# Loading one value weight in a thin and a wide column piece, and the first value projections by row blocks

## The chip, the cores and the metric

The kernel runs on one core of a Trainium2 chip. The core has five instruction streams that run side by side: TensorE (PE in the profile; its weight loads are listed as PEld), VectorE (DVE), ScalarE (ACT), GpSimd (POOL) and SyncE (SP). They meet through semaphores. Loads from memory are issued as DMAs from SyncE's or ScalarE's instruction stream and moved by 16 DMA engines that all streams share. The metric is the device time of one execution in microseconds (us); less is better.

## What is computed

The input `x` has 2048 rows of 512 columns, in bf16. Each row is normalized, and the result goes into two branches that are added to `x`.

```python
xn = layernorm(x)                                  # 2048 x 512
q, k, v = split(xn @ wqkv)                         # 32 heads of 16 columns each
phi(t) = [softmax(t @ w_phi), softmax(-t @ w_phi)] # per head, 32 features
kv = phi(k)^T v ;  z = sum over rows of phi(k)
o  = (phi(q) kv) / (phi(q) z + 1e-6)
A  = o @ wo                                        # linear attention
B  = ((xn @ w_gate) * (xn @ w_up)) @ w_down        # 1792 hidden columns
out = x + A + B
```

## The kernel before

The 2048 rows are 16 row tiles of 128 rows, numbered 0 to 15, and four groups of four. In the code `n` is a row tile, and `c` or `j` is one of the four blocks of 128 input columns (DC is 4). The weight for v is the last third of `wqkv`. It lies on chip as `wv[128, 4, 512]`: `wv[:, j, :]` holds its rows 128 j to 128 j + 127, which is what the j-th matmul of a row tile reads. P is 128, D is 512, DH is 16.

All matrix products of a row tile need the tile transposed: `xnT` holds, for each column block, 128 columns of the input down the partitions and the rows along. The first four tiles are transposed on TensorE (`lt`, line 202: four 128x128 transposes into one PSUM bank, then one copy by ScalarE into `xnT`), the other twelve by DMA later on.

**The order of the work** is written out by hand: the engines' streams hold the instructions in the order in which the code issues them, and an instruction that waits holds up all behind it on its engine. The stretch around the change is the start of the kernel, in this order on each engine:

- SyncE issues the loads, lines 82 to 95: x tile 0, x tile 2, wv's column blocks j = 0, 1 (`dma_wv(0, 2)`), wv's j = 2, 3 (`dma_wv(2, DC)`), then pieces of the gate and up weights, `w_phi`, a transposing load of the k weights, and so on.
- ScalarE issues x tile 1 and x tile 3 (lines 102 and 103). Its first computation that waits for data is line 376, which sums each row of x tile 1 into `tots[1]`. Behind it in its stream stand the copies of the transposed tiles (line 206), two for tile 0 (each of two column blocks) and one for each of tiles 1 to 3.
- VectorE sums tile 0 (line 373) and writes `xns[0]` = 512 x minus its row sum in two halves (line 337); then `xns[1]`, which needs ScalarE's sum; then sum and difference of tile 2 and of tile 3; then the variances of the four tiles (line 340).
- TensorE starts with eight matmuls on constants (`warm_up`, line 311; the last one is a quarter as long), so that it is in use before data is there. Then come the transposes and the first value projections, `first_v(n, js)` (line 353): `first_v(n, js)` adds, for row tile n, the matmuls of the column blocks js into one PSUM bank. Tiles 0 and 1 use the two banks that later gather `kv`; tiles 2 and 3 take one of six rotating banks.

The order on TensorE is that of lines 380 to 397:

```python
lt(0, 0, 2); lt(0, 2, DC)
warm_up(2, 1)
first_v(0, (0,))
lt(1)
first_v(0, (1,))
lt(2)
first_v(0, (2, 3))
first_v(1, range(DC))
lt(3)
first_v(2, range(DC))
first_v(3, range(DC))
```

That is 16 matmuls of 512 columns and 16 transposes. Behind them follow `ffn(3)`, three units of eight matmuls each (lines 274 and 278), which read the gate and up weights and `xnT` of all four tiles, and then the rest of the kernel, some 206 us of mostly TensorE work.

Of the kernel before, what the change touches and what calls it, by code (L numbers as in the profile page):

```python
# [21 lines left out]
def kernel(  # L22
# [12 lines left out]
    nc = tc.nc  # L35
    P = 128
    S, D = A_x.shape[-2], A_x.shape[-1]
    F = B_w_gate.shape[-1]
    H = 32
    DH = D // H  # L40
    NT = S // P
    DC = D // P
# [15 lines left out]
    wv = wpool.tile([P, DC, D], BF16)  # L58
# [9 lines left out]
    def dma_x(lo, hi, eng=nc.sync):  # L68
        eng.dma_start(out=xall[:, lo:hi, :], in_=x_view[:, lo:hi, :])  # L69
# [1 line left out]
    def dma_cols(eng, w, src, lo, hi, at=0):  # L71
        eng.dma_start(out=w[:, :, lo - at:hi - at], in_=src[:, lo:hi].rearrange("(c p) f -> p c f", p=P))

    def dma_wv(lo, hi):
        nc.sync.dma_start(out=wv[:, lo:hi, :],
                          in_=A_wqkv[lo * P:hi * P, 2 * D:3 * D].rearrange("(c p) f -> p c f", p=P))

    def dma_gu(lo, hi):
        dma_cols(nc.sync, wg, B_w_gate, lo, hi)
        dma_cols(nc.sync, wu, B_w_up, lo, hi)  # L80

    dma_x(0, 1)
    dma_x(2, 3)
    dma_wv(0, 2)
    dma_wv(2, DC)
    dma_gu(0, 2 * P)
    nc.sync.dma_start(out=wphi[:], in_=A_w_phi.rearrange("(c h) d f -> (h d) c f", c=DC))
    dma_gu(2 * P, 5 * P)
# [10 lines left out]
    ones = nc.const_aps.tensor(1.0, [P, P], BF16)  # L99
    first = consts.tile([P, 1], BF16)  # L100
    nc.scalar.activation(out=first[:], in_=ones[:, 0:1], func=AF.Exp, scale=1.0)
    dma_x(1, 2, nc.scalar)
    dma_x(3, 4, nc.scalar)
    ident = consts.tile([P, P], BF16)
    make_identity(nc, ident[:])
    mhalf = consts.tile([P, GT], F32)
# [38 lines left out]
    def bank(name, dt=F32, n=TT):  # L145
        return ps_s.tile([P, n], dt, name=name, tag="s")
# [55 lines left out]
    def lt(n, lo=0, hi=DC):  # L202
        tp = bank("tp", BF16).rearrange("p (c t) -> p c t", c=DC)
        for c in range(lo, hi):
            nc.tensor.transpose(out=tp[:, c, :], in_=xns[n][:, c * P:(c + 1) * P], identity=ident[:])  # L205
        nc.scalar.copy(out=xnT[:, lo:hi, n * P:(n + 1) * P], in_=tp[:, lo:hi, :])  # L206
# [27 lines left out]
    def proj(ps, n, w, js=range(DC)):  # L234
        for j in js:
            nc.tensor.matmul(ps, lhsT=xnT[:, j, n * P:(n + 1) * P], rhs=w[:, j, :],  # L236
                             start=(j == 0), stop=(j == DC - 1))
# [68 lines left out]
    def warm_up(k, reps=DC):  # L306
        for _ in range(k):
            nc.tensor.matmul(warm[:, 0:reps * P], lhsT=ones,
                             rhs=nc.const_aps.tensor(1.0, [P, reps * P], BF16), start=True, stop=True)
# [4 lines left out]
    with tc.tile_pool(name="ps_k", bufs=1, space=PSUM) as ps_k:  # L314
# [21 lines left out]
        def sub_sum(n, tot, lo=0, hi=D):  # L336
            nc.vector.tensor_scalar(out=xns[n][:, lo:hi], in0=xall[:, n, lo:hi], scalar1=float(D), scalar2=tot[:],
                                    op0=ALU.mult, op1=ALU.subtract)
# [14 lines left out]
        def first_v(n, js):  # L353
            if n not in vps:
                vps[n] = kvbank[n][:] if n < 2 else bank("pv")
            proj(vps[n], n, wv, js)
# [15 lines left out]
        def sum_of(n):  # L372
            nc.vector.tensor_reduce(out=tots[n][:], in_=xall[:, n, :], axis=AX.X, op=ALU.add)
# [5 lines left out]
        sub_sum(1, tots[1])  # L379
        lt(0, 0, 2)  # L380
        lt(0, 2, DC)
        warm_up(2, 1)
        first_v(0, (0,))
        lt(1)
        first_v(0, (1,))
        for n in (2, 3):
            sum_of(n)
            sub_sum(n, tots[n])
        lt(2)
        first_v(0, (2, 3))  # L390
        first_v(1, range(DC))
        lt(3)
        first_v(2, range(DC))
        for n in (2, 3, 0, 1):
            stats_of(n)
            scales_of(n, float(D))
# [125 lines left out]
```

## Time and profile before

| what | value |
|---|---|
| time, median of 3 runs (lowest to highest) | 221.18 us (221.09 to 223.44) |
| time of the profiled execution | 221.23 us |
| its span, first to last instruction | 219.5 us |
| TensorE busy | 214.5 us, 98% of the span |
| VectorE, ScalarE, GpSimd busy | 141.0, 89.4, 74.1 us |
| granted TensorE clock | 0.999 |
| TensorE idle between 4.71 and 5.97 us | 1.26 us |

The profile shows one execution. Times within it count from its first instruction, and the measured time is 1.7 us longer than the span. A row of the timeline gives the start, the length of the stretch, the engine, the line of the kernel, the operation, what it writes and reads, the shapes, the count, and, in brackets, how long the engine had been idle before it and what ended that. A row with a count above 1 is a run of instructions that overlap or follow one another. A matmul of 512 columns has a latency of 379 ns in the profile, while the next one starts 216 ns later, so lengths overlap. DMA rows give the kilobytes and the time from issue to landing.

### The profile page before, as it was taken

The page shows a single profiled execution, that of the slowest core. Times are in us where ns is not written, and L with a number is a line of the kernel's source. Part 1 is how long each engine was busy: PE and PEld are TensorE (multiplying, and loading weights), DVE is VectorE, ACT ScalarE, POOL GpSimd, SP SyncE. Part 2 cuts the span into 40 slices and gives each one's busy share as a digit, 9 for nine tenths or more (in the row PEclk, how much of TensorE's full clock was granted, in tenths as well). Part 3 has the DMA queues.
Part 4 walks back from the last instruction along what each step waited for, and adds up shares of the span by engine and source line. Part 5 has one row for each costly group of instructions (what it writes and reads, how often), then busy time and mean ns, then how long its engine had stood idle before and what let it go on. Part 6 is the DMA issues. An engine that isn't in the chain of part 4 may idle for free.

```text
span 219.5 us, 3489 instructions
## 1 busy us (share of the span) xinstructions
PE 214.5 (98%) x1292; PEld 102.8 (47%) x1292; DVE 141.0 (64%) x239; ACT 89.4 (41%) x159; POOL 74.1 (34%) x71
## 2 busy tenths in 40 slices
PE   6999999999999999999999999999999999999994
PEld 2444445454444444444544444444444444444443
DVE  5858866886598757667499773196655645454321
ACT  5546586459665875465434222141231322100000
POOL 2540853363348463636045433033023033000000
PEclk9999999999999999999999999999999999999999
DMA  5999996102202431202018445114451431512301
GB/s 176 283 293 371 375 242 93 42 0 51 48 0 49 50 75 21 48 3 48 1 30 98 92 106 115 47 24 96 96 75 24 96 72 27 97 48 72 74 25 48
DMA packets 48529, 19.91 MB, mean 91 GB/s; under 512 B 37504, under 2 KB 48512, under 8 KB 48512
## 3 DMA queue, kind: packets, MB, share of 16 engines
q1 hardware_dynamic: 48224, 19.42, 39.8%
q10 hardware_dynamic: 288, 0.26, 0.4%
q8 instruction: 10, 0.16, 0.3%
q14 instruction: 7, 0.06, 0.1%
HBM read 8.67 MB, written 2.10 MB: 49 GB/s over the span
## 4 chain that ended last, share of the span: by engine, by line
PE 96%; DMA 2%; SPq 0%; DVE 0%; issue 0%
PE g L274 22%; PE fin L290 22%; PE u L278 22%; PE fin L293 6%; PE k L236 6%; PE q L236 6%; PE pv L236 6%; DMA wv<-in_A_wqkv_dram 2%; PE kv L330 2%; PE ab L461 2%; PE kv L236 1%; PE pq L225 1%; SPq L69 0%; PE tp L205 0%; DVE o_sb L300 0%
## 5 line engine op out<-in xcount | busy, mean ns | idle before, releaser
L274 PE MATMUL g<-xnT,wg 128*128 128x512 bf16 x224 | 57.5, 379 | 0.0
L278 PE MATMUL u<-xnT,wu 128*128 128x512 bf16 x224 | 57.5, 379 | 0.0
L282 DVE TENSOR_TENSOR hT<-u,g_sb 128x512 bf16<-128x512 f32 x56 | 37.0, 666 | 24.9 <-PE u L278 16.8
L253 POOL TENSOR_TENSOR phiq<-e,rsum 128x1024 bf16<-128x1024 f32 x16 | 30.9, 1933 | 63.5 <-DVE rsum L251 56.0
L281 ACT CAST g_sb<-g 128x512 bf16<-128x512 f32 x56 | 32.8, 587 | 47.1 <-PE g L274 46.9
L249 DVE TENSOR_REDUCE sums<-e 128x64 f32<-128x1024 f32 x32 | 38.9, 1216 | 20.1 <-ACT e L246 20.1
L290 PE MATMUL fin<-wd,hT 128*128 128x512 bf16 (+2 forms) x238 | 51.1, 366 | 0.0
L253 POOL TENSOR_TENSOR phik<-e,rsum 128x1024 bf16<-128x1024 f32 x16 | 30.9, 1932 | 40.6 <-DVE rsum L251 38.5
L278 PEld LDWEIGHTS <-wu 128*128 128x128 bf16 x224 | 21.9, 98 | 26.4
L290 PEld LDWEIGHTS <-hT 128*128 128x128 bf16 x238 | 22.4, 98 | 24.8
L274 PEld LDWEIGHTS <-wg 128*128 128x128 bf16 x224 | 21.1, 98 | 24.0
L236 PEld LDWEIGHTS <-xnT 128*128 128x128 bf16 x192 | 17.4, 97 | 18.4 <-ACT xnT L206 0.9
L300 DVE TENSOR_TENSOR o_sb<-fin,xall 128x512 bf16<-128x512 f32 (+2 forms) x13 | 8.5, 650 | 20.5 <-PE fin L293 20.5
L251 DVE RECIPROCAL rsum<-sums 128x64 f32<-128x64 f32 x32 | 17.7, 553 | 3.1
L293 PE MATMUL fin<-wo,oT 128*128 128x512 bf16 (+2 forms) x68 | 16.6, 366 | 0.0
L236 PE MATMUL k<-W1k,xnT 128*128 128x512 bf16 x64 | 16.4, 379 | 0.0
L236 PE MATMUL q<-W1q,xnT 128*128 128x512 bf16 x64 | 16.4, 378 | 0.0
L245 ACT ACTIVATE e<-q 128x512 f32<-128x512 f32 x12 | 7.2, 597 | 22.2 <-PE q L236 22.2
L236 PE MATMUL pv<-wv,xnT 128*128 128x512 bf16 x56 | 14.2, 379 | 0.0
L474 DVE TENSOR_TENSOR otok<-ab,rden 128x512 bf16<-128x512 f32 x16 | 11.1, 692 | 0.6
L322 ACT CAST vt<-pv 128x512 bf16<-128x512 f32 x12 | 7.0, 587 | 10.0 <-PE pv L236 10.0
L153 DVE BATCH_NORM_STATS2 stats<-xall 128x6 f32<-128x512 bf16 x16 | 10.6, 665 | 0.0
(61 smaller groups left out, 130.4 us busy)
## 6 DMA issues: line engine op xcount, KB each, us to landing
out_dram<-o_sb SPq DMA_DIRECT2D x15, 128.0 KB, 2.0
wd<-in_B_w_down_dram SPq DMA_DIRECT2D x1, 1792.0 KB, 15.6
xall<-in_A_x_dram SPq DMA_DIRECT2D x1, 1024.0 KB, 11.6
wg<-in_B_w_gate_dram SPq DMA_DIRECT2D x1, 640.0 KB, 8.6
wu<-in_B_w_up_dram SPq DMA_DIRECT2D x1, 640.0 KB, 9.8
wv<-in_A_wqkv_dram SPq DMA_DIRECT2D x2, 256.0 KB, 4.4
xall<-in_A_x_dram SPq DMA_DIRECT2D x1, 512.0 KB, 4.2
wg<-in_B_w_gate_dram SPq DMA_DIRECT2D x1, 512.0 KB, 5.4
```

The source lines that it names most:

```text
L153: nc.vector.bn_stats(out=stats[:], in_=xall[:, n, :])
L236: nc.tensor.matmul(ps, lhsT=xnT[:, j, n * P:(n + 1) * P], rhs=w[:, j, :], start=(j == 0), stop=(j == DC - 1))
L249: nc.vector.tensor_reduce(out=sums[:], in_=ev, axis=AX.X, op=ALU.add)
L251: nc.vector.reciprocal(out=rsum[:].rearrange("p a b -> p (a b)"), in_=sums[:])
L253: nc.gpsimd.tensor_tensor(out=phi[:].rearrange("p g (x f) -> p (g x) f", f=DH), in0=ev, in1=rsum[:].to_broadcast((P, 2 * H, DH)), op=ALU.mult)
L274: nc.tensor.matmul(gps, lhsT=wg[:, c, f * P:(f + 1) * P], rhs=xnT[:, c, T * TT:(T + 1) * TT], start=(c == 0), stop=(c == DC - 1))
L278: nc.tensor.matmul(ups, lhsT=wu[:, c, f * P:(f + 1) * P], rhs=xnT[:, c, T * TT:(T + 1) * TT], start=(c == 0), stop=(c == DC - 1))
L281: nc.scalar.copy(out=g_sb[:], in_=gps)
L282: nc.vector.tensor_tensor(out=hTs[T][:, f, :], in0=ups, in1=g_sb[:], op=ALU.mult)
L290: nc.tensor.matmul(ps, lhsT=hTs[T][:, f, t4 * P:(t4 + 1) * P], rhs=wd[:, f, lo:lo + w], start=(f == 0), stop=False)
L293: nc.tensor.matmul(ps, lhsT=oTs[n][:, c, :], rhs=wo[:, c, lo:lo + w], start=False, stop=(c == DC - 1))
L474: nc.vector.tensor_tensor(out=o_tok[:].rearrange("p (b h d) -> p b h d", b=2, d=DH), in0=abv[:, :, :, 0:DH], in1=rden[:].to_broadcast((P, ...
```

## The change

The load of `wv` is cut by columns as well. Columns 0 to 15 of all four column blocks (512 runs of 32 bytes) are one DMA, issued first in ScalarE's queue, ahead of x tile 1. The remaining 496 columns are loaded by SyncE in two halves as before. x tile 3 moves from ScalarE's queue to SyncE's. SyncE's order becomes x tile 0, wv's j = 0, 1 (columns 16 on), x tile 2, x tile 3, wv's j = 2, 3 (columns 16 on), and then the same loads as before. On TensorE the first projections are ordered by row blocks of `wv`: j = 0, 1 of tiles 0, 1 and 2, then j = 2, 3 of the same tiles. The two short warm-up matmuls of 128 columns behind tile 0's transposes become one of 512 columns.

```diff
-    def dma_wv(lo, hi):
-        nc.sync.dma_start(out=wv[:, lo:hi, :],
-                          in_=A_wqkv[lo * P:hi * P, 2 * D:3 * D].rearrange("(c p) f -> p c f", p=P))
+    def dma_wv(lo, hi, f0, f1, eng=nc.sync):
+        eng.dma_start(out=wv[:, lo:hi, f0:f1],
+                      in_=A_wqkv[lo * P:hi * P, 2 * D + f0:2 * D + f1].rearrange("(c p) f -> p c f", p=P))
...
     dma_x(0, 1)
+    dma_wv(0, 2, DH, D)
     dma_x(2, 3)
-    dma_wv(0, 2)
-    dma_wv(2, DC)
+    dma_x(3, 4)
+    dma_wv(2, DC, DH, D)
     dma_gu(0, 2 * P)
...
     nc.scalar.activation(out=first[:], in_=ones[:, 0:1], func=AF.Exp, scale=1.0)
+    dma_wv(0, DC, 0, DH, nc.scalar)
     dma_x(1, 2, nc.scalar)
-    dma_x(3, 4, nc.scalar)
...
         lt(0, 0, 2)
         lt(0, 2, DC)
-        warm_up(2, 1)
+        warm_up(1)
         first_v(0, (0,))
         lt(1)
         first_v(0, (1,))
+        first_v(1, (0, 1))
         for n in (2, 3):
             sum_of(n)
             sub_sum(n, tots[n])
         lt(2)
-        first_v(0, (2, 3))
-        first_v(1, range(DC))
+        first_v(2, (0, 1))
+        for n in range(2):
+            first_v(n, (2, 3))
         lt(3)
-        first_v(2, range(DC))
+        first_v(2, (2, 3))
         for n in (2, 3, 0, 1):
             stats_of(n)
             scales_of(n, float(D))
```

## The prediction

> **What bounds the kernel now.** I read the busy times of the whole span first, then busy times by stretch, then the waits of the first 11 us, then the timeline of the start engine by engine.
>
> ```profile
> span 219.5 us, 3489 instructions
> ...
> PE 214.5 (98%) x1292; PEld 102.8 (47%) x1292; DVE 141.0 (64%) x239; ACT 89.4 (41%) x159; POOL 74.1 (34%) x71
> ```
>
> ```profile
> 0.00:4.71 4.71, 3.81 (x14) 1.36 (x14) 2.11 (x11) 2.48 (x6) 1.59 (x9) 1.00 0.54 158
> 4.71:5.97 1.26, 0.00 (x0) 0.10 (x1) 1.22 (x3) 0.37 (x2) 0.00 (x0) 1.00 0.94 300
> 5.97:10.10 4.13, 4.12 (x29) 2.10 (x29) 3.54 (x10) 2.26 (x4) 2.27 (x6) 1.00 1.20 305
> 10.10:217.00 206.90, 206.55 (x1251) 99.27 (x1249) 134.13 (x217) 84.29 (x150) 70.25 (x56) 1.00 0.39 84
> ```
>
> Behind the bounds and the length of a stretch stands PE's busy time. PE is the bound: from 10.10 us, where the first `ffn` matmul starts, it is busy 206.55 of 206.90 us. Nothing behind that point can absorb a delay, and the change touches only what lies ahead. So the forecast is one number: when does that first `ffn` matmul start? Before, at 10.10. From 5.97 on, PE does not stop; its one real hole is 4.71 to 5.97, and it waits there for wv:
>
> ```profile
> PE kv L236 <- DMA wv<-in_A_wqkv_dram: 1.3, 1, 1.3
> ```
>
> PE's timeline:
>
> ```profile
> 5.97 0.38 PE L236 MATMUL kv<-wv,xnT 128*128 128x512 bf16 x1 [1.26 <-DMA wv<-in_A_wqkv_dram]
> 6.19 0.38 PE L205 MATMUL tp<-ident,xn 128*128 128x128 bf16 x4
> 6.41 0.38 PE L236 MATMUL kv<-wv,xnT 128*128 128x512 bf16 x1
> 6.63 0.39 PE L205 MATMUL tp<-ident,xn 128*128 128x128 bf16 x4
> 6.85 1.46 PE L236 MATMUL kv<-wv,xnT 128*128 128x512 bf16 x6
> 8.14 0.39 PE L205 MATMUL tp<-ident,xn 128*128 128x128 bf16 x4
> 8.37 1.89 PE L236 MATMUL pv<-wv,xnT 128*128 128x512 bf16 x8
> ```
>
> Paces: eight matmuls from 8.37 to 10.10 give 0.216 us each; four transposes from 8.14 to 8.37 give 0.22.
>
> The row that matters most is how soon a transposed tile can be used. PE's weight loads and ScalarE's timeline:
>
> ```profile
> 4.86 0.10 PEld L236 LDWEIGHTS <-xnT 128*128 128x128 bf16 x1 [0.33 <-ACT xnT L206]
> ...
> 7.25 0.56 PEld L236 LDWEIGHTS <-xnT 128*128 128x128 bf16 x4 [0.30 <-ACT xnT L206]
> ...
> 9.21 0.56 PEld L236 LDWEIGHTS <-xnT 128*128 128x128 bf16 x4 [0.30 <-ACT xnT L206]
> ```
>
> ```profile
> 3.31 0.63 ACT L376 ACTIVATE junk<-xall 128x512 bf16<-128x512 bf16 x1 [1.03 <-DMA xall<-in_A_x_dram]
> 3.85 0.19 ACT L376 ACTIVATION_READ_ACCUMULATOR junk<-xall 128x1 f32 x1
> 4.44 0.65 ACT L206 COPY xnT<-tp 128x256 bf16<-128x256 bf16 x2 [0.40 <-PE tp L205]
> ```
>
> Tile 1's transposes start at 6.19 and its first weight load, held by ScalarE's copy, is at 7.25; tile 3's are 8.14 and 9.21. So 1.07 us pass, 1.09 with 0.02 to the matmul. **Before, this lag is filled**: behind tile 1's transposes stand one matmul, tile 2's transposes and two matmuls (0.22 + 0.22 + 0.22 + 0.43 = 1.09); behind tile 3's stand their own 0.22 and four matmuls (1.08).
>
> **The change, part by part.**
>
> *The order on PE.* PE takes its stream in order. Call *a* the start of tile 1's transposes. Afterwards tile 1's transposes and tile 0's j = 1 fill 0.43 of the 1.09 up to tile 1's first matmul: a hole of 0.66. Two matmuls (0.43), then tile 2's transposes at a + 1.52. Directly behind stands tile 2's j = 0, which needs them: 1.09 again, 0.22 filled, a hole of 0.87; the ready matmuls of tiles 0 and 1 (j = 2, 3) are queued behind it. Then six matmuls (1.30) to tile 3's transposes at a + 3.91. Behind these only two matmuls remain before tile 3 itself: 1.09 with 0.22 + 0.43 filled, a hole of 0.44. Tile 3's four matmuls take 0.86. The first `ffn` matmul is thus at **a + 5.86**; the new holes sum to 1.97 us, against 1.26 that could be won. To break even, *a* would have to be 4.24.
>
> *When is a?* Ahead of it stands tile 0's j = 0 (0.22), which needs wv's j = 0 and tile 0's first copy. ScalarE issues that copy behind the row sum of x tile 1. With x1 landing at L: sum starts L + 0.02 (landed 0.84 + 2.4, started 3.31), ends 0.73 later (3.31 to 4.04), copy 0.03 on, weight load 0.42 after the copy's start (4.44 to 4.86), matmul 0.03 on: L + 1.23, and a = L + 1.45. Even with x1 as before, the copy starts at 4.44 after the transposes, so the matmul is at 4.89 and a = 5.11 at best: `ffn` at 10.97, 0.87 late. VectorE is not later than this: `xns[1]` is ready 0.5 us after the sum; tile 2's sum and difference take 1.1 us more and have 1.5.
>
> *x1's landing.* ScalarE's queue issues the 16 columns first:
>
> ```profile
> wphi<-in_A_w_phi_dram SPq DMA_DIRECT2D x1, 16.0 KB, 5.1
> ```
>
> This load of `w_phi` has the same form (512 runs of 32 bytes), and its issue takes 0.51 us on SP's timeline. x1 is then issued at about 1.38 instead of 0.84. Lower bound of L: 3.3, as before, if the DMA engines and not the issue set it. Nearest upper row: x tile 3, today second in this queue behind 128 KB, issued at 1.25, landed 2.9 later at 4.15; with 0.13 more, 4.3. What is ahead of x1 now is 16 KB, in 512 packets of 9 ns each in the packet records of `w_phi` over 16 engines, so 0.3 us per engine. I take 4.0 (3.8 from the issue alone, 4.3 from x3). Then a = 5.45, `ffn` at **11.31, 1.2 us late**.
>
> [...]
>
> *wv's landing.* Before it was issued at 1.71 and landed 4.2 later at 5.94. Now its first half is second in SP's queue, issued at 1.24 (0.47 sooner), with x2's and x3's 256 KB no longer ahead: some 0.8 us at the 305 GB/s of the stretches' rows. Between 4.7 and 5.5; tile 0's first matmul is not ready before 5.23, so I take it as hidden, and it costs up to 0.3 if not. PE's first projection now waits for two DMAs, with all of PE's stream behind it. The second half of wv is needed at a + 4.0, after 9; it landed at 6.7 before.
>
> *The rest.* SP issues one more load (x3, 0.45 us) ahead of all later ones. The first gate weights landed at 7.6 for a use at 10.1, the k weights at 12.8 for a use at 15.4; each has over 2 us of cover, and PE is later too. One warm-up matmul of 0.22 instead of 0.11 lies in PE's hole: nothing. Statistics and copies of the projections move with PE.
>
> **Sum.** 221.23 + 1.2 = 222.4 us; the profiled execution lies 0.05 above the median, which I leave out.
>
> **Rivals.**
>
> 1. *Forecast, the holes of the new order* (0.63): +0.9 to +1.6, 222.4.
> 2. *Data late as well* (0.20). PE would be held by wv or x1. If wv still landed at 5.94, a = 6.19 and `ffn` at 12.05, +1.95. If x1 slipped to 5.0, because the first touch of wv's rows now goes ahead of it in its queue, a = 6.45, +2.2. Around 223.3. For: wv took 4.2 us where x1 took 2.4. Against: it had more ahead of it.
> 3. *PE's clock falls* (0.05). At the start, seven warm-up matmuls step by 0.43 us (0.82 to 3.77), twice the 0.216 later, for some 3.3 us. Three holes in 6 us could bring that back for as long: +1.2 + 1.65, 224.1. Against: the hole of 1.26 before did not. [...]
> 4. *Faster* (0.06): the wait for wv goes and no hole replaces it, 221.23 − 1.26 = 220.0. It needs *a* under 4.24, or the lag of 1.09 well under 0.7; against it stand the weight loads at 7.25 and 9.21, both held by ScalarE's copy.
> 5. *Nothing* (0.06): holes and gain cancel, 221.2.
>
> **Range and chances.** 221.4 to 223.5 holds the forecast with both ends of L and nearly all of rival 2; rivals 3, 4 and 5 are left out. A difference of 1% (2.2 us) is about what a measurement of this kernel can tell from no change. Forecast, 4 and 5 are within it, 3 is over it, 2 about half: slower by over 1% 0.15, faster by over 1% 0.02, within 0.83.
>
> **What would show it.** Right: PE's first projection between 5.1 and 5.6, released by ScalarE's copy; then three holes of about 0.66, 0.87 and 0.44 ended by `xnT` copies; first `ffn` matmul near 11.3; behind it the same 206.9 us to the same point. Wrong: that matmul at or before 10.1, a first projection still held by wv, matmul steps of 0.43 behind 5 us, or a new wait of PE past `ffn`.

## The result, and the profile after

The changed kernel is slower: a median of 223.15 us over 22 runs (222.84 to 225.51) against 221.86 us for the kernel before over 22 runs beside it (220.91 to 223.44). The ratio is 1.0083, with a 95% interval of 1.0056 to 1.0110. The two medians differ by 1.29 us; the ratio, taken on the median shown before the prediction, 221.18, is about 1.8 us. The forecast was 1.2.

Both kernels' times fall into groups. The changed kernel has 12 runs from 222.8 to 223.2, 4 from 224.0 to 224.4 and 6 from 225.4 to 225.5. The kernel before has 11 from 220.9 to 221.6, one at 222.2 and 10 from 222.8 to 223.4. What the groups are was the second question of this study. Group against group the loss is larger than the medians say: the lowest group has a median of 222.93 after and 221.24 before, 1.69 us apart. The profiled execution of the changed kernel is one of its longest, 225.51 us. Its page, first lines:

```profile
span 223.8 us, 3465 instructions
...
PE 217.2 (97%) x1267; PEld 103.9 (46%) x1291; DVE 141.1 (63%) x239; ACT 89.4 (40%) x159; POOL 74.1 (33%) x71
```

The span is 4.3 us longer. The waits of its first 20 us have no entry for wv any more. In its place stand TensorE's waits for ScalarE's copies of the transposed tiles, and ScalarE's wait for x tile 1 has grown from 1.0 us to 2.4 (total, times, longest):

```profile
ACT junk L377 <- DMA xall<-in_A_x_dram: 2.4, 1, 2.4
...
PE kv L237 <- ACT xnT L207: 0.8, 2, 0.5
...
PE pv L237 <- ACT xnT L207: 0.7, 1, 0.7
```

TensorE's timeline of the same execution:

```profile
5.70 0.61 PE L237 MATMUL kv<-wv,xnT 128*128 128x512 bf16 x1 [0.54 <-ACT xnT L207]
6.10 0.63 PE L206 MATMUL tp<-ident,xn 128*128 128x128 bf16 x4
6.53 0.63 PE L237 MATMUL kv<-wv,xnT 128*128 128x512 bf16 x1
7.42 1.03 PE L237 MATMUL kv<-wv,xnT 128*128 128x512 bf16 x2 [0.25 <-ACT xnT L207]
8.24 0.63 PE L206 MATMUL tp<-ident,xn 128*128 128x128 bf16 x4
9.56 1.03 PE L237 MATMUL pv<-wv,xnT 128*128 128x512 bf16 x2 [0.68 <-ACT xnT L207]
10.38 1.91 PE L237 MATMUL kv<-wv,xnT 128*128 128x512 bf16 x4
12.09 0.63 PE L206 MATMUL tp<-ident,xn 128*128 128x128 bf16 x4
```

Two things show at once. Two of the three holes of the new order are there, ahead of the rows at 7.42 and 9.56, each ended by a copy (line 207 is the old 206). And four matmuls from 10.38 take 1.91 us to the end of the last one, 1.71 us to the next row: 0.43 us each instead of 0.22. TensorE is at half rate up to about 13 us. The first `ffn` matmul starts at 14.28 instead of 10.10, and from there to the last matmul of the kernel 206.34 us pass in both profiles (to 220.62 after, to 216.43 before). So nothing behind the start changed, and the start is 4.18 of the 4.28 us between these two executions.

Two more profiled executions of the changed kernel followed, without an edit.

> The changed kernel once more, for another profiled execution. Theory (holes and late x tile 1 at full clock, the clock on top in some executions): at 222.9 us matmul steps of 0.22 us from 6 us on and the first ffn matmul at 11.7 to 11.8; at 224.1 steps of 0.43 us for part of the stretch and that matmul near 13.0; behind it 206.3 us to the last matmul in each. Rival: another wait behind the first ffn matmul makes the difference between the times.

> The same again: the first ffn matmul at 11.7 to 11.8 in an execution at 222.9 us, near 13.0 at 224.1, near 14.3 at 225.4, and 206.3 us behind it; by the rival another wait behind that matmul.

One took 224.30 us, the other 223.01. The second is the changed kernel at full clock from its first projection on. Its TensorE timeline:

```profile
5.75 0.39 PE L237 MATMUL kv<-wv,xnT 128*128 128x512 bf16 x1 [0.65 <-ACT xnT L207]
5.98 0.39 PE L206 MATMUL tp<-ident,xn 128*128 128x128 bf16 x4
6.20 0.38 PE L237 MATMUL kv<-wv,xnT 128*128 128x512 bf16 x1
7.04 0.61 PE L237 MATMUL kv<-wv,xnT 128*128 128x512 bf16 x2 [0.46 <-ACT xnT L207]
7.49 0.39 PE L206 MATMUL tp<-ident,xn 128*128 128x128 bf16 x4
8.55 0.60 PE L237 MATMUL pv<-wv,xnT 128*128 128x512 bf16 x2 [0.68 <-ACT xnT L207]
8.99 1.03 PE L237 MATMUL kv<-wv,xnT 128*128 128x512 bf16 x4
9.86 0.39 PE L206 MATMUL tp<-ident,xn 128*128 128x128 bf16 x4
10.08 0.59 PE L237 MATMUL pv<-wv,xnT 128*128 128x512 bf16 x2
10.92 1.04 PE L237 MATMUL pv<-wv,xnT 128*128 128x512 bf16 x4 [0.25 <-ACT xnT L207]
11.79 1.03 PE L275 MATMUL g<-xnT,wg 128*128 128x512 bf16 x4
```

By the starts, with 0.22 us for a matmul or four transposes, the holes are 6.42 to 7.04, 7.71 to 8.55 and 10.51 to 10.92: 0.62, 0.84 and 0.41. The first `ffn` matmul is at 11.79. In the execution of 224.30 us it is at 13.06. There TensorE was at full rate, lost it, and got it back:

```profile
6.21 0.38 PE L237 MATMUL kv<-wv,xnT 128*128 128x512 bf16 x1
...
9.00 1.04 PE L237 MATMUL pv<-wv,xnT 128*128 128x512 bf16 x2 [0.68 <-ACT xnT L207]
9.83 1.46 PE L237 MATMUL kv<-wv,xnT 128*128 128x512 bf16 x4
11.13 0.39 PE L206 MATMUL tp<-ident,xn 128*128 128x128 bf16 x4
```

The last matmul comes 206.34 us behind the first `ffn` matmul in both. The three groups of the changed kernel are therefore 11.8, 13.1 and 14.3 us of start, and what separates the three profiled executions is how long TensorE runs at half rate. The clock records kept with the traces give the times: in the 225.51 us execution full rate came only at 13.32 us; in the 224.30 us execution it came at 3.87, was gone from 7.29 to 10.70, and came back; in the 223.01 us execution no step behind 5.75 is at half rate.

### The profile page after: what moved, and what is told of

The parts are those of the page before. It is cut to its first block, busy times and chain, and to the rows that moved or that the text cites. A ratio compares the mean times of both kernels' runs of the same rounds, so it can differ in the third digit from the quotient of the medians.

```text
span 223.8 us, 3465 instructions
## 1 busy us (share of the span) xinstructions
PE 217.2 (97%) x1267; PEld 103.9 (46%) x1291; DVE 141.1 (63%) x239; ACT 89.4 (40%) x159; POOL 74.1 (33%) x71
## 4 chain that ended last, share of the span: by engine, by line
PE 95%; DMA 1%; ACT 1%; issue 1%; DVE 0%
PE u L279 22%; PE fin L291 22%; PE g L275 21%; PE fin L294 6%; PE q L237 6%; PE k L237 6%; PE pv L237 6%; PE ab L464 2%; PE kv L331 2%; PE kv L237 1%; DMA xall<-in_A_x_dram 1%; ACT xnT L207 1%; PE tp L206 1%; PE pq L226 1%; ACT junk L377 0%
## 5 line engine op out<-in xcount | busy, mean ns | idle before, releaser
L279 PE MATMUL u<-xnT,wu 128*128 128x512 bf16 x221 | 56.8, 379 | 0.2
L275 PE MATMUL g<-xnT,wg 128*128 128x512 bf16 x213 | 56.3, 379 | 0.6
L237 PE MATMUL pv<-wv,xnT 128*128 128x512 bf16 x56 | 15.3, 396 | 0.7 <-ACT xnT L207 0.7
L237 PE MATMUL k<-W1k,xnT 128*128 128x512 bf16 x61 | 15.8, 379 | 0.0
```

The costliest lines, as they stand in the source:

```text
L275: nc.tensor.matmul(gps, lhsT=wg[:, c, f * P:(f + 1) * P], rhs=xnT[:, c, T * TT:(T + 1) * TT], start=(c == 0), stop=(c == DC - 1))
L279: nc.tensor.matmul(ups, lhsT=wu[:, c, f * P:(f + 1) * P], rhs=xnT[:, c, T * TT:(T + 1) * TT], start=(c == 0), stop=(c == DC - 1))
```

## The experiments

### The two halves of the change, one at a time

`order_only` has the loads of before and the new order:

```diff
 first_v(0, (1,))
+first_v(1, (0, 1))
 ...
 lt(2)
-first_v(0, (2, 3))
-first_v(1, range(DC))
+first_v(2, (0, 1))
+for n in range(2):
+    first_v(n, (2, 3))
 lt(3)
-first_v(2, range(DC))
+first_v(2, (2, 3))
```

> The kernel before, with only the new order of the first projections on TensorE (row blocks j = 0, 1 of tiles 0 to 2 first); the loads and the two short warm-up matmuls stay. Theory (the new order leaves holes behind the transposes): the first projection stays at 5.97 us, held by wv; tile 1's transposes start at 6.19, the first ffn matmul at 6.19 + 5.86 = 12.05 instead of 10.10, about +1.9 us against before, where the clock is released at the same time. Rival (only the loads cost; the order is neutral): ffn at 10.1 and the time of before. Rival of the clock (holes keep TensorE at half rate): matmul steps of 0.43 us behind 6 us in some executions, then over +3 us.

Measured: 225.7 us median over 6 runs (224.18 to 226.92), ratio 1.0146 (1.0098 to 1.0193). The first `ffn` matmul of its profile is at 13.69. Its TensorE timeline shows the clock turned down in between (half rate from 8.37 to 11.78 by the clock records):

```profile
6.61 0.38 PE L205 MATMUL tp<-ident,xn 128*128 128x128 bf16 x4
6.83 0.38 PE L236 MATMUL kv<-wv,xnT 128*128 128x512 bf16 x1
7.67 0.60 PE L236 MATMUL kv<-wv,xnT 128*128 128x512 bf16 x2 [0.46 <-ACT xnT L206]
8.11 0.39 PE L205 MATMUL tp<-ident,xn 128*128 128x128 bf16 x4
9.18 1.04 PE L236 MATMUL pv<-wv,xnT 128*128 128x512 bf16 x2 [0.68 <-ACT xnT L206]
10.01 1.91 PE L236 MATMUL kv<-wv,xnT 128*128 128x512 bf16 x4
```

Two matmuls from 7.67 are done in 0.60 us (full rate), two from 9.18 take 1.04 (half rate). So this run has holes and clock mixed, and does not price the order by itself.

`loads_only` has the changed kernel's loads with the order and warm-up of before.

> The changed kernel's loads (16 columns of wv on ScalarE's queue ahead of x tile 1, x tile 3 on SyncE's) with the order of the projections and the warm-up of before. Theory (the loads do bring the first projection forward, the order gives it back): x tile 1 lands at 4.6, the first projection is at 5.7, behind it 4.13 us of dense work as before, the first ffn matmul at 9.8 and the time 0.3 us under before. Rival (the late x tile 1 is the loss): 0.5 us or more over before, with a new wait of TensorE behind the first projection.

Measured: 221.81 us median (7 of 12 runs from 221.55 to 221.84, five at 222.8 to 223.3), ratio 1.0011 (0.9980 to 1.0042). The expectation was too kind. The first projection did come forward, to 5.60, but TensorE then stopped twice: tile 2's transposes wait for VectorE, which got its sum of tile 1 late, and tile 0's j = 2 waits for the second half of wv, which landed at 7.3:

```profile
6.71 0.40 PE L206 MATMUL tp<-ident,xn 128*128 128x128 bf16 x4 [0.28 <-DVE xn L338]
7.34 1.46 PE L237 MATMUL kv<-wv,xnT 128*128 128x512 bf16 x6 [0.23 <-DMA wv<-in_A_wqkv_dram]
```

Its first `ffn` matmul is at 10.58, against 10.10 and 10.39 in the two full-clock executions of the kernel before, and its lower group of times (median 221.62) lies with that of before beside it (221.55). Together: the loads take the long wait for wv away and hand back all that they win, and the order adds holes of its own.

### Holding the clock still

If the holes also keep TensorE's clock low, their price must be read at full rate. `filled` is the changed kernel with more matmuls on constants in the holes:

```diff
-warm_up(1)
+warm_up(2)
 first_v(0, (0,))
 lt(1)
 first_v(0, (1,))
+warm_up(1)
 first_v(1, (0, 1))
 ...
 lt(2)
+warm_up(2)
 first_v(2, (0, 1))
```

> The changed kernel with four more warm-up matmuls of 512 columns put into TensorE's holes (one ahead of the first projection, one behind tile 0's j = 1, two behind tile 2's transposes). Theory of the clock (the executions of the changed kernel at 224.1 and 225.4 us are those in which TensorE stays at half rate until 13 us, since the holes leave it too little in use): those times vanish or get rare, and the median goes to the lowest level, 222.9. Rival (the clock's release does not hang on the holes): the same spread as the changed kernel, or a little longer from the extra matmuls.

Measured: 12 runs from 222.91 to 223.25, median 223.05. The groups at 224 and 225.4 are gone (10 of 22 runs of the changed kernel lie there). The added matmuls stand in the holes and cost nothing: the first `ffn` matmul of this profile is at 11.78, against 11.79 in the full-clock execution of the changed kernel. So those two groups are the clock, and a fuller TensorE removed them.

```profile
7.70 0.60 PE L309 MATMUL warm<-const-bfloat16-1.0 128*128 128x512 bf16 x2
8.54 0.60 PE L237 MATMUL pv<-wv,xnT 128*128 128x512 bf16 x2 [0.24 <-ACT xnT L207]
...
11.78 1.03 PE L275 MATMUL g<-xnT,wg 128*128 128x512 bf16 x4
```

`order_filled` prices the order alone in the same way: loads of before, new order, `warm_up(3)` ahead of the first projection, and the same fillers of one and two matmuls in the holes.

> The loads of before and the new order, with warm-up matmuls in TensorE's holes (three of 512 columns ahead of the first projection, one behind tile 0's j = 1, two behind tile 2's transposes), so that the clock cannot hide what the order costs. Theory of the holes: first projection 6.0 to 6.4, then 0.22 to tile 1's transposes and 5.86 more to the first ffn matmul, 12.1 to 12.5, about 1.9 us over the lowest times of before (223.1), in nearly all executions. Rival (the order costs nothing at full clock, order_only was slow only by the clock): the lowest times of before, 221.2.

Measured: 12 runs from 223.14 to 223.59, median 223.4, first `ffn` matmul at 12.38. That is 2.0 us over the lower group of before beside it (median 221.4), and no run is as long as any of `order_only`'s. The kernel before with the same three constant matmuls ahead of its first projection (`before_filled`, below) took 221.46 us beside it, with that matmul at 10.33; so the order alone costs 1.94 us, 2.05 by that matmul. Its timeline:

```profile
6.02 0.63 PE L236 MATMUL kv<-wv,xnT 128*128 128x512 bf16 x1
6.44 0.51 PE L205 MATMUL tp<-ident,xn 128*128 128x128 bf16 x4
...
7.63 0.60 PE L236 MATMUL kv<-wv,xnT 128*128 128x512 bf16 x2 [0.25 <-ACT xnT L206]
...
9.14 0.61 PE L236 MATMUL pv<-wv,xnT 128*128 128x512 bf16 x2 [0.24 <-ACT xnT L206]
```

From tile 1's transposes (6.44) to the first `ffn` matmul are 5.94 us, of which some 0.13 are transposes still at half rate (full rate came at 6.69). The rival that priced the order at nothing is out.

### Which part of the loads makes x tile 1 late

`no_cols` is the changed kernel without the 16-column DMA:

```diff
-dma_wv(0, 2, DH, D)
+dma_wv(0, 2, 0, D)
 ...
-dma_wv(2, DC, DH, D)
+dma_wv(2, DC, 0, D)
 ...
-dma_wv(0, DC, 0, DH, nc.scalar)
 dma_x(1, 2, nc.scalar)
```

> The changed kernel, but wv comes in two whole halves on SyncE's queue again and x tile 1 is first on ScalarE's queue. Theory (the 512 short runs ahead of x tile 1 put it off from 3.3 to 4.6): x tile 1 lands by 3.4, the first projection is at 4.9 to 5.1, held by ScalarE's copy, the first ffn matmul 10.9 to 11.1, 0.8 us under the changed kernel and 0.9 over before. Rival (x tile 1 is put off by the traffic of wv on SyncE's queue, not by the short runs): landing still after 4.3 and the time of the changed kernel.

Measured: x tile 1 landed at 3.51, and 12 runs lie from 222.31 to 222.93, median 222.44: 0.5 us under the changed kernel's lowest group, where 0.8 were expected. Its profiled execution (222.88) is at half rate until 6.1 us, so its first `ffn` matmul at 11.72 is not one at full clock. `cols_behind` is cleaner; it is `filled` with the two DMAs of ScalarE's queue swapped, so the bytes and the short runs stay.

```diff
-dma_wv(0, DC, 0, DH, nc.scalar)
 dma_x(1, 2, nc.scalar)
+dma_wv(0, DC, 0, DH, nc.scalar)
```

> The filled version of the changed kernel with one edit: on ScalarE's queue x tile 1 goes first and the 16 columns of wv behind it. Same bytes, same short runs. Theory (it is the place ahead of x tile 1 that costs): x tile 1 lands at 3.3 to 3.5, the first projection is at 5.0 to 5.3 unless the 16 columns land later than that, the first ffn matmul at 11.1 to 11.4 and the time 0.4 to 0.6 us under the filled version (223.05). Rival (the short runs slow all loads wherever they stand): x tile 1 still lands after 4.2 or wv after 5.5, and the time of the filled version.

Measured: median 222.58 us (222.16 to 223.37), 0.5 under `filled`, though the two were not timed side by side. The profiles are the firmer ground. ScalarE's sum of x tile 1, in `cols_behind` and then in the changed kernel's full-clock execution:

```profile
3.67 0.63 ACT L377 ACTIVATE junk<-xall 128x512 bf16<-128x512 bf16 x1 [1.39 <-DMA xall<-in_A_x_dram]
```

```profile
4.71 0.63 ACT L377 ACTIVATE junk<-xall 128x512 bf16<-128x512 bf16 x1 [2.43 <-DMA xall<-in_A_x_dram]
```

The swap alone brings x tile 1 forward by 1.04 us and the first `ffn` matmul from 11.78 to 11.20; the rest of that microsecond is lost because tile 0's transposes wait for VectorE until 4.41, so that ScalarE's copy of them starts only at 4.73. The short runs hurt by their place ahead of x tile 1, not by being there. All profiles say the same: in the 13 with x tile 1 first in its queue this sum starts between 3.31 and 3.69, in the 6 with the 16 columns ahead of it between 4.45 and 4.73.

How they do it is settled only in part. The queue worked in order: in `cols_behind` the first short packet comes at 3.35, directly behind x tile 1's last. In the changed kernel's profiles the 512 short packets (9 ns each) take from 2.2 or 2.3 to 2.8 or 2.9, 0.5 to 0.8 us, not the 0.3 of the forecast: packets of SyncE's queue take 56% of the same engines' time meanwhile (2.2 to 2.9 us, execution of 225.51 us). x tile 1's first packet comes only at 3.3 to 3.4, 2 us after its issue at 1.32, where 1.3 us pass in the kernel before between the issue at 0.84 and the first packet at 2.14. The 0.4 to 0.5 us between the last short packet and x tile 1's first are not explained, and they are not needed for the loss: in `filled` the first packet comes at 2.95, without that pause, and x tile 1 lands at 4.69 all the same.

### Undoing the holes, and a better version

`repaired` keeps the changed kernel's loads, puts j = 2, 3 of tiles 0 and 1 directly behind tile 2's transposes again and tile 2 behind tile 3's, and has constant matmuls in the holes (two ahead of the first projection, one behind tile 0's j = 1):

```diff
 lt(2)
-first_v(2, (0, 1))
 for n in range(2):
     first_v(n, (2, 3))
 lt(3)
-first_v(2, (2, 3))
+first_v(2, range(DC))
```

> The changed kernel's loads, with the j = 2, 3 projections of tiles 0 and 1 put directly behind tile 2's transposes and tile 2's four projections behind tile 3's, as in the order of before, and two warm-up matmuls ahead of the first projection and one behind tile 0's j = 1. Theory of the holes: the holes of 0.87 and 0.44 us go, the one of 0.66 stays; with tile 1's transposes at 5.95 the first ffn matmul is at 5.95 + 4.55 = 10.5 and the time 1.3 us under the filled version (223.05), so 221.7. Rival (wv's second half, landing at 7.2 to 7.5, or x tile 2 takes the place of the holes): 222.3 or more, with a wait on a DMA or on VectorE's difference in the profile.

Measured: 12 runs from 221.56 to 221.96, median 221.68, first `ffn` matmul at 10.26. With the same loads, the two undone holes are worth 1.4 us (223.05 to 221.68, not timed side by side). From tile 1's transposes to the first `ffn` matmul the profiles say 5.81 in `filled` and 4.55 here, 1.26 us; by the forecast's steps it is 1.31. `repaired_no_cols` has the same order with `no_cols`' loads.

> The same order and warm-up as the repaired version, with wv in two whole halves on SyncE's queue and x tile 1 first on ScalarE's. Theory (x tile 1 lands at 3.4 and the first projection is at 5.0 to 5.3): tile 1's transposes at 5.4, first ffn matmul at about 9.9 to 10.1, time at or a little under the lowest of before (221.0 to 221.3) in nearly all executions. Rival (wv's second half, landing at 6.7 to 7.5, holds TensorE instead): first ffn matmul at 10.5 or later, 221.7.

Measured: 221.48 us (221.15 to 221.94), first `ffn` matmul at 10.49. Its first projection is at 5.19, but TensorE then waits for wv's second half (landed 7.6), which is what the rival said:

```profile
7.68 1.02 PE L236 MATMUL kv<-wv,xnT 128*128 128x512 bf16 x4 [0.37 <-DMA wv<-in_A_wqkv_dram]
```

`best` takes the order and the whole wv halves of `repaired_no_cols`, issues wv's second half ahead of x tile 3 and puts tile 1's transposes directly behind tile 0's; `best_x3` also returns x tile 3 to ScalarE's queue.

> A version meant to beat both: SyncE loads x tile 0, wv's first half, x tile 2, wv's second half, x tile 3; x tile 1 first on ScalarE's queue; tile 1's transposes directly behind tile 0's, then j = 0, 1 of tiles 0 and 1, tile 2's transposes, j = 2, 3 of tiles 0 and 1, tile 3's transposes, tiles 2 and 3; two warm-up matmuls behind tile 0's transposes, one behind tile 0's projections. Theory: tile 1's transposes at 5.0, its projections at 6.1, wv's second half by 6.8, first ffn matmul at 9.5 to 9.8, 220.7 to 220.9 us in nearly all executions. Rival (wv's second half lands after 7 here too): ffn at 10.3 or later, 221.4.

> The same as the version meant to beat both, with x tile 3 on ScalarE's queue behind x tile 1 as before. Theory: wv's second half is one load sooner in SyncE's queue but shares the engines with x tile 3; the same times, 220.7 to 220.9. Rival (x tile 3 ahead takes the engines from wv): wv's first half after 5, first ffn matmul 0.2 us or more later than in that version.

Measured: 221.35 us (220.87 to 221.62) and 221.27 us (220.74 to 223.17), ratios 0.9968 (0.9939 to 0.9997) and 0.9968 (0.9937 to 0.9999). `best` is no faster than the lower group of before beside it (median 221.35); what it gains is that the upper group is missing. Its first `ffn` matmul is at 10.24, not 9.5 to 9.8; its profiled execution runs at half rate until 5.9. `best_x3` reached 9.95 in its profile, and yet that execution took 223.17 us. That execution has a new wait far behind the start, at 33.6 us, for the DMA transpose of tile 4:

```profile
PE pv L236 <- DMA xnT<-xn: 1.9, 1, 1.9
```

That transpose stands in SyncE's queue behind the loads of the down and output weights (2.3 MB). It raised a rival for the kernel before: its upper group of times could be this wait too.

### What the two groups of the kernel before are

Four runs tell the two causes apart. `before_filled` changes only `warm_up(2, 1)` to `warm_up(3)`. `late_wd` leaves the start alone and issues wd and wo behind the DMA transposes of tiles 4 to 7. `before_2` and `before_3` are the kernel before, profiled again.

> The kernel before, with three warm-up matmuls of 512 columns instead of two of 128 in the hole ahead of the first projection; nothing else. Theory (the upper times of before, 222.8 to 223.4, are also executions in which TensorE's clock is released late, since the hole of 1.26 us counts as idle): these times vanish or get rare and the median goes to 221.3. Rival (the upper times of before have another cause, or the release hangs on its phase alone): the same two groups of times as before.

> The kernel before, with the loads of the down and output weights (wd, wo; first read at about 120 us) issued behind the four DMA transposes of tiles 4 to 7 on SyncE's queue instead of ahead of them; the start is untouched. Theory of the transposes (the upper times of before, 222.7 to 223.5, are executions in which TensorE waits some 2 us near 33.6 us for the transposed tile 4, whose DMA stands behind wd's and wo's bytes): the upper times vanish, median 221.3. Rival (the upper times come from TensorE's clock at the start): two groups of times as before, 221.3 and 223.

> The kernel before once more, for another profiled execution. If it falls in the upper group of times (over 222.6 us): by the theory of the transposes its first ffn matmul is at about 10.1 to 10.4 and TensorE waits for the transposed tile near 33.6 us; by the theory of the clock its matmuls step by 0.43 us behind 6 us and the first ffn matmul is at about 12.

> The same again: in an execution over 222.6 us the theory of the transposes has a wait near 33.6 us behind a first ffn matmul at 10.1 to 10.4, the theory of the clock matmul steps of 0.43 us behind 6 us. In an execution near 221.3 neither.

Measured: `before_filled` has 12 runs from 221.14 to 221.97, median 221.46; no run of the upper group. `late_wd` has six runs from 220.8 to 221.8 and six from 222.8 to 223.4: two groups as before; its profiled execution, 222.81 us, has no wait for the transposes and half rate until 9.4. `before_2` took 222.74 us, and its TensorE timeline is this:

```profile
5.85 0.58 PE L236 MATMUL kv<-wv,xnT 128*128 128x512 bf16 x1 [0.56 <-DMA wv<-in_A_wqkv_dram]
6.23 0.63 PE L205 MATMUL tp<-ident,xn 128*128 128x128 bf16 x4
6.65 0.63 PE L236 MATMUL kv<-wv,xnT 128*128 128x512 bf16 x1
7.08 0.63 PE L205 MATMUL tp<-ident,xn 128*128 128x128 bf16 x4
7.51 2.28 PE L236 MATMUL kv<-wv,xnT 128*128 128x512 bf16 x6
```

The steps are 0.43 us until about 9 (full rate came at 9.17), the first `ffn` matmul is at 11.58, and no wait follows. `before_3` took 221.56 us with full rate from 6.3 on and that matmul at 10.39. The upper group of the kernel before is the clock; the wait for the transposes is not in it. Of the 117 runs of the kernel before that were timed beside the experiments five lie higher still, at 224.5 to 224.8; none of them was profiled, and what they are is open.

`best_late_wd` joins `best_x3` and the later wd and wo:

```diff
-nc.sync.dma_start(out=wd[:], in_=B_w_down.rearrange("(c p) d -> p c d", p=P))
-nc.sync.dma_start(out=wo[:], in_=A_wo.rearrange("(c p) n -> p c n", p=P))
 ...
 nc.sync.dma_start(out=wT2[:, 0, :, :], in_=A_wqkv[:, 0:D], transpose=True)
+nc.sync.dma_start(out=wd[:], in_=B_w_down.rearrange("(c p) d -> p c d", p=P))
+nc.sync.dma_start(out=wo[:], in_=A_wo.rearrange("(c p) n -> p c n", p=P))
```

> The best_x3 version with the same move of wd and wo. Theory of the transposes: its two times of 223 do not come back and its times go to those of a first ffn matmul at 9.7 to 9.95, 220.8 to 221.0. Rival (clock): some executions at 223 remain.

Measured: 220.94 us median (220.87 to 221.60), ratio 0.9949 (0.9919 to 0.9979). No run is at 223, as the theory of the transposes expected; with two such runs among 12 of `best_x3`, that alone would not prove it. The version beats both kernels. Most of that gain against the median of before (221.58 beside it) is the upper group that is gone; against before's lower group (median 221.14) it is 0.2 us.

## Why the prediction was right or wrong

*The steps that failed.* The term that the sum had too small is L, the landing of x tile 1: taken as 4.0, measured 4.64 to 4.71. And the clock was taken to be the same in every execution, which neither kernel showed. Like for like, in the lowest groups and at full clock, the loss is 1.7 us, not 1.2. That the two medians differ by 1.29, close to the forecast, is luck: each is the median of a mixture of groups.

*The place and the sign.* Right. The wait for wv went, and ScalarE's copies took its place; nothing behind the first `ffn` matmul moved (206.34 us before and after).

*The holes of the order.* Right, and the largest term. Forecast 0.66, 0.87 and 0.44; measured 0.62, 0.84 and 0.41 at full clock. From tile 1's transposes to the first `ffn` matmul 5.86 were forecast; 5.81 were measured in the changed kernel and 5.94 in `order_filled`. The order alone cost 1.94 us between `before_filled` and `order_filled`, where the three forecast holes sum to 1.97.

*x tile 1's landing.* Here the sum failed. L was taken as 4.0, with ends at 3.3 and 4.3; measured 4.64 to 4.71, outside both ends and more than halfway to rival 2's 5.0. The first projection came at 5.70 to 5.76, past the 5.6 that was to show the forecast right. The upper row was x tile 3's landing, second in the same queue behind 128 KB, and I reasoned that 16 KB ahead must cost less. It cost more: neither the bytes nor 9 ns for each packet, 0.3 us in the forecast, account for it. The base was low too: 3.3 is one execution, and with the loads of before x tile 1 landed at 3.56 in `before_2` and 3.67 in `before_3`. In the full-clock execution (L 4.69) the error of 0.69 us was in part returned by two smaller ones: the first projection came 1.06 us behind the landing instead of 1.23, since ScalarE started the copy (5.34) before the sum's last step had ended (5.44), and the 5.86 was 5.81. Together 0.69 − 0.17 − 0.05 = 0.47, and the first `ffn` matmul was at 11.79 instead of the forecast 11.31: 1.7 us late where 1.2 were forecast. Equal bytes did not give an equal landing: `cols_behind`, with the bytes of `filled`, landed x tile 1 at 3.65 against 4.69, 1.04 us sooner, so the place in the queue decided.

*wv's landing.* Hidden behind x tile 1, as forecast, though the first half landed sooner than forecast: at 4.3 to 4.4 in three profiles, not 4.7 to 5.5. The second half is first read at *a* + 3.04 by the prediction's own steps, not at *a* + 4.0 (8.99 in the full-clock execution); it landed at 6.5 to 7.6, so the slip cost nothing.

*The clock.* The rival "PE's clock falls" was given 0.05, and 10 of the changed kernel's 22 runs lie 1.2 or 2.5 us above the 222.9 group, and the two executions of such lengths that were profiled show its sign, steps of 0.43 us behind 5 us. But a fall is only one way: the profiled execution of 225.51 us had not reached full rate before 13.32. Of the 10 runs, two have a mean granted clock under 1.00 (0.992 and 0.985), as the 224.30 us execution has, in which the clock did fall; the other eight read 1.00, as the execution of 225.51 us does. That these eight got full rate late is argued from that one profile. What the prediction missed is that the kernel before has it too. It argued that the hole of 1.26 us had not brought the half rate back, from one profiled execution with full rate from 3.87 us on; in `before_2` it came at 9.17, and 10 of 22 runs of before took 1.5 to 2.2 us more than its lower group. So the forecast stood on one of two cases of the kernel before, and the measured ratio compares two mixtures.

*The range.* It reached the median (223.5 against 223.15) only because the late data of rival 2 were let in; 10 of the 22 single runs lie above it. "Within 1%" fits the ratio of 1.0083, whose interval ends at 1.011. But the prediction held 1% to be about what a measurement can tell from no change; 22 runs of each kernel told 0.8% from none.

## What to carry to other kernels

When an engine takes its work in order, an earlier start is worth only what stays filled behind it (here the first projection came 0.22 us sooner, at 5.75 instead of 5.97, and the first `ffn` matmul 1.69 later, at 11.79 instead of 10.10, both at full clock): write down the lag from each producer to its first consumer and count the independent work that stands between them in the stream, before and after. Ahead of a small load that another engine's first instruction waits for, put nothing without measuring it, however few bytes it has (here 16 KB in 512 runs put x tile 1 off by 1.0 us). A kernel whose times fall into groups should be compared group by group, and a few matmuls on constants in TensorE's holes can be worth more than the reordering of the real ones (with three of them, in `before_filled`, none of 12 runs lay in the upper group, where 15 of 35 runs of the kernel before beside them did, from 222.65 to 223.50; `best_late_wd`, with its own order and loads, won 0.2 us against the lower group).

## What the runs showed of the hardware

- The granted clock of a page can hide half rate. It reads 1.00 in the execution of 225.5 us, whose matmuls step by 0.43 us until 13 us; the first clock record of that trace is at 13.32, and ahead of it only the steps show the rate. A later loss does show: in the 224.3 us execution it reads 0.64 from 7 to 8 us, 0.50 from 8 to 10 and 0.65 from 10 to 11, and 0.992 over the whole.
- The half rate came back with short holes, for 3.41 us each time. In `order_only` matmuls step by 0.23 us at 7.7 and by 0.40 at 9.2; in the 3.41 us before the loss at 8.37 the longest idle stretch on TensorE was 1.30 us, and it was busy for 48% of them. In the 224.3 us execution of the changed kernel it was 1.09 us and 55%. The kernel before, with one hole of 1.26 us and 61%, kept full rate in its profiled execution. Three stretches give no threshold, and whether single holes or the busy share decide is not shown. With the four constant matmuls of `filled` none of its 12 runs was in the upper groups.
- 512 runs of 32 bytes ahead of a 128 KB load in the same queue put its landing off by 1.0 us (3.65 in `cols_behind`, 4.69 in `filled`), although their packets take 9 ns each.
